# Preparing late q and k earlier, and splitting the last output product by columns, in a fused attention and MoE kernel

## The chip, the cores and the metric

The kernel runs on one core of one Trainium2 chip. The metric is the device time of one execution in microseconds (us). On one core there is no second die to compare with.

## The reference, cut to what matters

```python
# q, k, v: (4, 8, 768, 64) float32; lam: (8,); w_in: (512, 2048); w_out: (2048, 512)
for b in range(12):                      # blocks of 64 rows
    intra = (q_b k_b^T * decay mask) v_b
    inter = (q_b * lam_pow) kv_state
    out_b = intra + inter
    kv_state = lam_block * kv_state + (k_b * rev_pow)^T v_b
x = out as (3072, 512)                   # tokens x model
h = x @ w_in                             # (3072, 2048)
g = gelu_tanh(h)
return g @ w_out                         # (3072, 512) float32
```

Linear attention with decay, then a two-layer MLP over its output. In the kernel, attention is cut into 24 steps (a batch, 256 rows, half of the heads). The MLP's matrix products are queued as "filler" pieces, which are put between the dependent parts of the attention steps so that TensorE has work while other engines prepare the next step.

## The kernel before

Each step's q is scaled on VectorE (tile `qk`), its k is cast on ScalarE, its v is scaled on GpSimd (tile `v`), and from step 9 on a transposing transfer brings q and k into the layout for the scores. The loads of a step are issued behind the preparation of an earlier one. For step 10 they are split: v is issued right behind the transfer that transposes step 9.

```python
def prep_v(s):
    tv = a16p.tile([P, 2, HH, D], FP16, tag="v16", name=f"v16_{s}")
    pin(nc.gpsimd.tensor_tensor(wide(tv[:]), ld32[s][2][:], decay(dv, s), ALU.mult))
    a16[s] = a16[s] + (tv,)
    if s >= 6:
        if s + 3 == FIRST_DMA_T + 1:          # s == 7: step 10, q and k only
            load_step(s + 3, "qk")
        else:
            load_ahead(s + 3)

def prep_qk(s):
    ...
    pin(q_eng.tensor_tensor(wide(tq), q32[:], decay(dq, s), ALU.mult))
    ...
    if s >= FIRST_DMA_T:                      # FIRST_DMA_T = 9
        o = qkp.tile([P, 2, 2, 2, P], FP16, tag="qkT", name=f"qkT_{s}")
        pin(nc.sync.dma_start_transpose(...))
        qkT[s] = o
        if s == FIRST_DMA_T:
            load_step(s + 1, "v")             # v of step 10
```

The second MLP product is computed by seven half-size products of summed blocks (A to E are their PSUM banks, `gs` the sums of `g` that VectorE makes for them). Its very last product, bank E, is a 128x256 block over eight weight tiles; then one sum and one store:

```python
def product(m, p):
    ...
    dst = banks[name][:, half]
    t = slice(p * P, p * P + P)
    for i in range(HF):                       # HF = 8
        ...
        pin(nc.tensor.matmul(dst, lhsT, rhs, start=(i == 0), stop=(i == HF - 1), ...))
    ...
    elif final and m in (7, 6):
        ...
        d = o[:, T, T, :]
        pin(tt(d, banks[name][:, half], d, ALU.add))
        queue = nc.scalar if m == 7 else nc.sync
        pin(queue.dma_start(out=rows[:, T], in_=d))
```

The order of the late steps (`R` and `burst` are attention steps, `U` their state updates, `fill(n)` n pieces of the MLP):

```python
for n in range(8, 16):
    stage_t(n)
    prep_qk(n + 2) if n == 8 else prep(n + 2)
    fill(3 if n == 14 else 2)
    R(n, n - 1)
    ...
for n in range(16, NSTEP + 1, 2):             # NSTEP = 24
    if n + 2 < NSTEP:
        prep(n + 2)
    fill(2)
    burst((n, n + 1) if n < NSTEP else (), (15,) if n == 16 else (n - 2, n - 1))
    if n == NSTEP:
        break
    fill(2)
    U(n)
    U(n + 1)
    if n + 3 < NSTEP:
        prep(n + 3)
    fill(14 if n % 4 else 8)
fill(len(filler))
```

## Time and profile before

| | value |
|---|---|
| runs before the prediction | 203.87, 203.91 and 204.37 us |
| median | 203.91 us |
| run that was profiled | 204.35 us, span 202.6 us |
| TensorE busy | 194.3 us of the span |

The page cuts the span in 40 equal slices (about 5 us each) and gives each engine's busy share in tenths:

```profile
PE   6789999999999999999999999999999999999993
DVE  5896623889999989968799749889556471334753
```

TensorE (PE) has room only in the first three slices and the last. VectorE (DVE) is at 9 in many slices of the middle, and there its order of instructions can hold TensorE up for a few tenths of a microsecond. A finer table gives the busy time in chosen stretches. The columns here are TensorE matmuls, TensorE weight loads, VectorE, ScalarE, GpSimd, each with its number of instructions, then the granted clock, the share of the transfer engines and their rate:

```profile
60.00:66.00 6.00, 5.89 (x96) 4.67 (x94) 6.00 (x11) 2.32 (x6) 4.23 (x4) 1.00 1.22 231
66.00:72.00 6.00, 5.84 (x89) 5.08 (x90) 6.00 (x14) 3.22 (x7) 2.62 (x3) 1.00 1.23 271
130.00:140.00 10.00, 9.85 (x177) 8.65 (x175) 8.39 (x17) 3.98 (x9) 0.00 (x0) 1.00 0.09 18
```

VectorE is busy for all twelve microseconds from 60 to 72 us, and GpSimd for more than half of them. TensorE stands still for 0.27 us there and for 0.15 us between 130 and 140 us. Those are busy times with modelled ends, so the waits are read from the order of the chain rather than from these sums. The prediction shows that chain.

### The profile page before, as it was taken

How to read it: one execution, taken by the hardware profiler on the slowest of the kernel's cores; microseconds unless marked ns; L12 is line 12 of the kernel's file. 1: busy time of each engine (PE TensorE's matmuls, PEld its weight loads, DVE VectorE, ACT ScalarE, POOL GpSimd, SP SyncE). 2: the span in 40 equal slices, each digit the busy share in tenths (PEclk: the TensorE clock that was granted, in tenths of full speed). 3: DMA queues.
4: the chain of work that ended last, by engine and by line, in shares of the span. 5: the costliest groups of instructions: out<-in, count | busy, mean ns of one | idle time of the engine just before them, and what ended most of it. 6: DMA issues, size and time to landing. Idle time of an engine off the chain costs nothing.

```text
span 202.6 us, 5666 instructions
## 1 busy us (share of the span) xinstructions
PE 194.3 (96%) x2348; PEld 129.9 (64%) x2348; DVE 145.4 (72%) x293; ACT 107.8 (53%) x205; POOL 66.3 (33%) x80
## 2 busy tenths in 40 slices
PE   6789999999999999999999999999999999999993
PEld 1456544456888888654688764688664688545882
DVE  5896623889999989968799749889556471334753
ACT  2465778375993473487642378524367414466210
POOL 6594132457358254162541609203402000000000
PEclk9999999999999999999999999999999999999999
DMA  6999999999999999999975999305510003300014
GB/s 173 290 328 389 383 387 377 289 292 308 345 256 220 266 207 240 204 271 166 239 193 115 282 230 208 70 0 130 133 58 3 0 0 107 104 0 0 3 45 162
DMA packets 64202, 37.85 MB, mean 187 GB/s; under 512 B 17585, under 2 KB 59569, under 8 KB 64177
## 3 DMA queue, kind: packets, MB, share of 16 engines
q1 hardware_dynamic: 63344, 36.97, 72.1%
q10 hardware_dynamic: 832, 0.52, 0.8%
q8 instruction: 18, 0.29, 0.6%
q14 instruction: 8, 0.06, 0.1%
HBM read 27.26 MB, written 6.29 MB: 166 GB/s over the span
## 4 chain that ended last, share of the span: by engine, by line
PE 77%; DVE 11%; SPq 4%; DMA 4%; issue 2%; ACT 1%; DVEq 0%
PE Hps L484 34%; PE MD L555 7%; PE MB L555 7%; PE O2ps L499 7%; PE MA L555 7%; DVE gs L531 4%; SPq L70 4%; DMA wi<-in_moe_w_in_dram 4%; PE MC L555 3%; PE Hps L601 3%; PE S L295 2%; DVE qk L243 2%; DVE PT L305 2%; PE OK L353 1%; PE Tps L266 1%
## 5 line engine op out<-in xcount | busy, mean ns | idle before, releaser
L484 PE MATMUL Hps<-xT,w_in 128*128 128x512 f16 (+1 forms) x416 | 78.7, 346 | 0.0
L488 ACT ACTIVATE gT<-Hps 128x512 f16<-128x512 f32 x88 | 52.3, 597 | 29.5 <-PE Hps L484 28.5
L484 PEld LDWEIGHTS <-w_in 128*128 128x128 f16 x416 | 40.3, 98 | 33.7
L531 DVE TENSOR_TENSOR gs<-gT 128x1024 f16<-128x1024 f16 (+1 forms) x62 | 39.9, 699 | 18.5 <-ACT gT L488 18.5
L456 POOL TENSOR_TENSOR u<-t,lumask 128x256 f16<-128x256 f32 x40 | 29.4, 747 | 67.8 <-DVE t L449 49.8
L555 PEld LDWEIGHTS <-gs 128*128 128x128 f16 x400 | 38.9, 98 | 5.0 <-DVE gs L531 0.5
L305 DVE TENSOR_TENSOR PT<-S,mask 128x512 f16<-128x512 f32 x48 | 30.4, 681 | 9.5 <-PE S L295 9.5
L230 POOL TENSOR_TENSOR v<-v,dv 128x512 f16<-128x512 f32 x24 | 28.5, 1193 | 4.9 <-PE S L295 1.7
L555 PE MATMUL MA<-w_sum,gT 128*128 128x256 f16 x160 | 19.5, 273 | 0.4 <-DVE o L587 0.3
L555 PE MATMUL MB<-w_out,gs 128*128 128x256 f16 x160 | 19.1, 273 | 0.0
L555 PE MATMUL MD<-w_sum,gs 128*128 128x256 f16 x152 | 18.6, 273 | 0.3 <-DVE gs L531 0.3
L562 ACT ACTIVATE m<-MB 128x512 f32<-128x512 f32 x10 | 6.0, 597 | 23.9 <-PE MB L555 23.9
L248 ACT ACTIVATE qk<-k 128x512 f16<-128x512 f32 x24 | 15.0, 626 | 6.8 <-DMA k<-in_k_dram 6.8
L243 DVE TENSOR_TENSOR qk<-q,dq 128x512 f16<-128x512 f32 x23 | 18.5, 803 | 0.0
L555 PEld LDWEIGHTS <-gT 128*128 128x128 f16 x160 | 15.4, 98 | 3.5 <-ACT gT L488 0.5
L430 ACT ACTIVATE xT<-OK 128x256 f16<-128x256 f32 x29 | 11.2, 455 | 8.0 <-PE OK L353 7.7
L499 PE MATMUL O2ps<-w_out,gT 128*128 128x512 f16 x64 | 14.6, 379 | 0.0
L566 DVE TENSOR_TENSOR o<-MA,m 128x512 f32<-128x512 f32 x10 | 6.9, 688 | 10.2 <-ACT m L562 10.2
L128 DVE TENSOR_TENSOR w_sum<-w_out 128x1024 f16<-128x1024 f16 x10 | 8.9, 932 | 6.4 <-POOL w_out L118 3.5
L430 ACT ACTIVATE xT<-O 128x256 f16<-128x256 f32 x18 | 6.4, 458 | 10.2 <-PE O L404 7.9
L295 PEld LDWEIGHTS <-qkT 64*64 64x64 f16 x384 | 6.0, 106 | 7.0 <-issue 3.2
L449 DVE SCALAR_TENSOR_TENSOR t<-t,lamu,OK 128x64 f32<-128x64 f32 x44 | 10.1, 273 | 0.5
(68 smaller groups left out, 168.7 us busy)
## 6 DMA issues: line engine op xcount, KB each, us to landing
q<-in_q_dram SPq DMA_DIRECT2D x24, 256.0 KB, 5.2
k<-in_k_dram SPq DMA_DIRECT2D x24, 256.0 KB, 5.2
v<-in_v_dram SPq DMA_DIRECT2D x23, 256.0 KB, 5.3
out_dram<-o SPq DMA_DIRECT2D x22, 256.0 KB, 4.5
wo<-in_moe_w_out_dram SPq DMA_DIRECT2D x4, 1024.0 KB, 9.5
wi<-in_moe_w_in_dram SPq DMA_DIRECT2D x4, 512.0 KB, 7.8
wi<-in_moe_w_in_dram SPq DMA_DIRECT2D x2, 1024.0 KB, 12.8
v<-in_v_dram ACTq DMA_DIRECT2D x1, 256.0 KB, 4.3
```

Of the source, the lines that this page charges most:

```text
L230: pin(nc.gpsimd.tensor_tensor(wide(tv[:]), ld32[s][2][:], decay(dv, s), ALU.mult))
L243: pin(q_eng.tensor_tensor(wide(tq), q32[:], decay(dq, s), ALU.mult))
L248: pin(nc.scalar.activation(out=wide(tk), in_=k32[:], func=AF.Copy))
L305: pin(nc.vector.tensor_tensor(t[:, hl].rearrange("p b c d -> p b (c d)"), Sps[:].rearrange("p b c d -> p b (c d)"), mask[:].unsqueeze(1).t ...
L430: pin(nc.scalar.activation(out=d, in_=o, func=AF.Copy))
L449: pin(nc.vector.scalar_tensor_tensor(t[:, hp, :], state[half][:, hp, :], lamu[:, 2 * half + hp : 2 * half + hp + 1], K[:, hp, :], ALU.mult ...
L456: pin(nc.gpsimd.tensor_tensor(u[:], state[half][:].unsqueeze(2).to_broadcast([P, 2, 2, D]), lumask[:, 2 * half : 2 * half + 2, :].unsqueez ...
L484: pin(nc.tensor.matmul(by_block(Hps[:, i, :]), w_in16[:, c, f * P : (f + 1) * P], x(c), start=(c == 0), stop=(c == NC - 1)))
L488: pin(nc.scalar.activation(out=dst, in_=Hps[:], func=AF.Gelu_apprx_tanh))
L499: pin(nc.tensor.matmul(O2[tau][0][:], gT[:, f % HF, f // HF, tau * P : (tau + 1) * P], w_out16[:, f, :], start=(n == 0), stop=(n == NF - 1)))
L531: pin(nc.vector.tensor_tensor(gsum[m][:, i, :], block(T0, F0, i), block(T1, F1, i), op))
L555: pin(nc.tensor.matmul(dst, lhsT, rhs, start=(i == 0), stop=(i == HF - 1), skip_group_check=True))
```

## The change

Its intent is threefold.
- In step 9 one filler piece goes ahead of the preparation of step 11, so that a sum that TensorE waits for (`gs`) stands ahead of the `qk` product of step 11 on VectorE.
- In the last stretch the even steps 20 and 22 are prepared earlier among the filler pieces instead of right ahead of their burst. Step 18 stays where it was.
- The very last product is made in two halves of 128 columns, each with its own PSUM bank, sum and store.

```diff
@@ product()
+                if name == "E":
+                    banks["E2"] = ps_M.tile([P, P], FP32, tag="M", name="ME2")
...
-            for i in range(HF):
+            parts = [slice(0, P), slice(P, HE)] if name == "E" else [slice(0, HE)]
+            for cols, i in [(cols, i) for cols in parts for i in range(HF)]:
...
-                d = o[:, T, T, :]
-                pin(tt(d, banks[name][:, half], d, ALU.add))
-                queue = nc.scalar if m == 7 else nc.sync
-                pin(queue.dma_start(out=rows[:, T], in_=d))
...
+                    sums = [(parts[0], dst0[:, 0:P], nc.scalar), (parts[1], banks["E2"][:], nc.sync)]
+                for cols, part, queue in sums:
+                    d = o[:, T, T, cols]
+                    pin(tt(d, part, d, ALU.add))
+                    pin(queue.dma_start(out=rows[:, T, cols], in_=d))
@@ the order of the steps
         stage_t(n)
+        fill(1 if n == 9 else 0)
         prep_qk(n + 2) if n == 8 else prep(n + 2)
-        fill(3 if n == 14 else 2)
+        fill({9: 1, 14: 3}.get(n, 2))
...
-    for n in range(16, NSTEP + 1, 2):
-        if n + 2 < NSTEP:
-            prep(n + 2)
-        fill(2)
-        burst((n, n + 1) if n < NSTEP else (), (15,) if n == 16 else (n - 2, n - 1))
...
+    prep(18)
+    fill(2)
+    for n in range(16, NSTEP, 2):
+        burst((n, n + 1), (15,) if n == 16 else (n - 2, n - 1))
         fill(2)
         U(n)
         U(n + 1)
-        if n + 3 < NSTEP:
-            prep(n + 3)
-        fill(14 if n % 4 else 8)
+        for m in (n + 3, n + 4):
+            if m < NSTEP:
+                prep(m)
+            fill(4 if m % 2 == 0 and n % 4 == 0 else 6 if m % 2 == 0 else 6 if n % 4 == 0 else 10)
+    burst((), (NSTEP - 2, NSTEP - 1))
```

More of the change, by code (lines that the diff above doesn't have):

```diff
@@ L545, in product @@
                 banks[name] = ps_M.tile([P, 2, HE], FP32, tag="M", name=f"M{name}")
-            dst = banks[name][:, half]
+                if name == "E":
+                    banks["E2"] = ps_M.tile([P, P], FP32, tag="M", name="ME2")
+            dst = dst0 = banks[name][:, half]
             t = slice(p * P, p * P + P)
-            for i in range(HF):
+            parts = [slice(0, P), slice(P, HE)] if name == "E" else [slice(0, HE)]
+            for cols, i in [(cols, i) for cols in parts for i in range(HF)]:
                 lhsT = block(*G_PLAIN[m], i)[:, t] if m in G_PLAIN else gsum[m][:, i, t]
@@ L554, in product @@
                     rhs = w_sum16[:, w_slot[m], i, :]
-                pin(nc.tensor.matmul(dst, lhsT, rhs, start=(i == 0), stop=(i == HF - 1),
+                if cols.start:
+                    dst = banks["E2"]
+                pin(nc.tensor.matmul(dst[:, 0 : cols.stop - cols.start] if name == "E" else dst,
+                                     lhsT, rhs[:, cols], start=(i == 0), stop=(i == HF - 1),
                                      skip_group_check=True))
@@ L580, in product @@
                 rows = out[row : row + P, :].rearrange("q (e d) -> q e d", e=2)
-                d = o[:, T, T, :]
-                pin(tt(d, banks[name][:, half], d, ALU.add))
-                queue = nc.scalar if m == 7 else nc.sync
-                pin(queue.dma_start(out=rows[:, T], in_=d))
+                if m == 7:
+                    sums = [(slice(0, HE), banks[name][:, half], nc.scalar)]
+                else:
+                    sums = [(parts[0], dst0[:, 0:P], nc.scalar), (parts[1], banks["E2"][:], nc.sync)]
[3 more added lines that the diff above has]
+                    pin(queue.dma_start(out=rows[:, T, cols], in_=d))
             elif m == 6:
@@ L790 @@
         fill(2 if n in (8, 11, 15) else 3)
-    for n in range(16, NSTEP + 1, 2):
-        if n + 2 < NSTEP:
-            prep(n + 2)
-        fill(2)
-        burst((n, n + 1) if n < NSTEP else (), (15,) if n == 16 else (n - 2, n - 1))
-        if n == NSTEP:
-            break
+    prep(18)
+    fill(2)
+    for n in range(16, NSTEP, 2):
+        burst((n, n + 1), (15,) if n == 16 else (n - 2, n - 1))
         fill(2)
```

## The prediction

> **What bounds the kernel now.** I read first the busy shares by engine, then the chain that ended last in order of time, then the timeline around each place where that chain leaves TensorE, and last the stores at the very end. The page says
>
> ```profile
> PE 194.3 (96%) x2348; PEld 129.9 (64%) x2348; DVE 145.4 (72%) x293; ACT 107.8 (53%) x205; POOL 66.3 (33%) x80
> ```
>
> The span is 202.6 us and TensorE is busy for 194.3 of it at full granted clock, so a change can only win the few places where TensorE stands still, or the stretch after its last product. The list of what TensorE's matmuls and weight loads waited for gives no wait over 1.5 us, and after 60 us only waits of 0.2 to 0.5 us. The chain names those that the change can touch:
>
> ```profile
> 65.50 0.61 DVE gs L531
> 66.11 0.05 issue
> 66.16 1.05 PE MD L555 x8
> ...
> 106.91 0.45 issue
> 107.36 0.70 DVE o L587
> 108.06 0.04 issue
> 108.10 1.91 PE MA L555 x16
> ...
> 119.96 0.55 PE O L404 x8
> ...
> 136.57 0.70 DVE o L587
> 137.27 0.04 issue
> 137.31 0.44 PE K L393 x31
> ```
>
> Columns: start, length, what. Three times TensorE resumes the moment a VectorE instruction ends: at 66.16, 108.10 and 137.31 us. Between 67.2 and 99 us, and from 138 us to its end, the chain is TensorE almost unbroken. The timelines there:
>
> ```profile
> 62.01 2.94 POOL L230 TENSOR_TENSOR v<-v,dv 128x512 f16<-128x512 f32 x2
> 63.97 1.53 DVE L243 TENSOR_TENSOR qk<-q,dq 128x512 f16<-128x512 f32 x1
> 65.42 0.68 DVE L531 TENSOR_TENSOR gs<-gT 128x1024 f16<-128x1024 f16 x1
> 69.78 0.68 DVE L587 TENSOR_TENSOR o<-MD,o 128x512 f32<-128x512 f32 x1
> 70.68 4.53 PE L484 MATMUL Hps<-xT,w_in 128*128 128x256 f16 x40
> ...
> 135.97 0.68 DVE L243 TENSOR_TENSOR qk<-q,dq 128x512 f16<-128x512 f32 x1
> 136.57 0.69 DVE L587 TENSOR_TENSOR o<-MD,o 128x512 f32<-128x512 f32 x1
> ```
>
> In both places a qk product (the preparation of a later step's q) stands in VectorE's order just ahead of the instruction TensorE needs. At the end:
>
> ```profile
> 199.25 0.42 DVE L582 TENSOR_TENSOR o<-ME,o 128x256 f32<-128x256 f32 x1 [0.45 <-PE ME L555]
> 199.71 0.36 SPq L584 DMA_DIRECT2D out_dram<-o  x1
> ```
>
> Last product, 0.42 us sum, store; then 2.9 us until the span ends. In tenths of a microsecond the DMA share is full from 198.6 to 200.4, dips to 0.43 at 200.5, is full again at 200.7 and gone at 201.1.
>
> **What the Trainium skill says.** (1) "Perfetto Trace Analysis", Optimizing Scalar/DVE Operations: GpSimd and VectorE share an SBUF read port. The trace agrees: the qk product took 1.53 us while GpSimd made its v, against 0.68 us at 135.97 with GpSimd idle. (2) "TensorE: Matmul & The Clock Gate", Back-to-back issue gap: in a stream of weight load and matmul pairs both set the pace, about 81 ns a pair at 128 columns. Here it is a little quicker: 8 such pairs in 0.55 us (the O line above), 69 ns; 256 columns take 109 ns. So half the columns do not cost half the time. (3) "PSUM — Partial Sum Buffer", PSUM bank collisions raise a hardware error: two engines must not touch one bank in the same quadrants at once. That is why the half product needs a second bank before VectorE may read the first; this trace cannot show it. (4) "DMA: Bandwidth & Descriptors", Anatomy of one DMA: most of a transfer's fixed cost is the receipt from the memory written. The trace agrees in kind: data stop at 201.1 us, the span ends at 202.6.
>
> **Part 1, step 9: one piece of filler ahead of the preparation of step 11.** TensorE's order is unchanged by it; on VectorE the sum gs_6 and the product qk_11 change places. Before, the eight MD matmuls that start at 64.85 us last 8 x 109 ns = 0.87, so the next eight could start at 65.72; they started at 66.16, after gs_6 (65.42 to 66.10). Loss 0.44 us. With gs_6 in qk_11's place at 63.97, and slowed by GpSimd as the qk was (or less, as 16-bit sums before it were slowed by about half), it ends by 65.1 to 65.4, in time: TensorE gains up to 0.44 there. Not all must survive: VectorE is busy 10.0 of 10 us between 60 and 70, and its total work is the same. TensorE next needs it for banks: the Hps of 70.68 waits in the program for the o sum that ran 69.78 to 70.46, slack 0.22 us. If VectorE is no faster overall, only 0.22 survive; if the sum loses less to GpSimd than the qk did (qk lost 1.53 - 0.68 = 0.85), more. After that VectorE has idle time waiting on TensorE's results (0.74 us at 76.0), so what survives 71 us stays. I take **0.33 us**.
>
> **Part 2, q and k of steps 20 and 22 earlier, of 18 not.** Filler between bursts adds up as before (12 and 18 pieces), so TensorE's order stays. qk_20 moves two pieces up, but VectorE's order does not change around it and TensorE waits for nothing at that burst (118.6 us): 0. qk_22 moves from between the o sums to ahead of three gs sums. Then the o sum of L587 starts when its product ends, some 136.15 rather than 136.57, and ends about 136.85. TensorE's K would have followed its first matmul at 136.97 and now resumes at 137.31: gain **0.34 us**. The three gs sums move back 0.6 to 0.7 us; in the old order they are done, in steps, at about 131.9, 132.6 and 133.2, and their products start at 133.5, 134.4 and 135.2, so at 132.6, 133.3 and 133.9 they are still in time. The wait at 108.10 has qk_18 in front of it, and its place is unchanged: it stays. From 138 us nothing else stops TensorE, so 0.34 goes to the end.
>
> **Part 3, the last product in halves.** TensorE: 16 pairs of 69 ns, 1.10 us, for 8 of 109 ns, 0.87: **0.23 us added**. First half done 0.55 us after the start, second 1.10. A sum of 128 columns: 512 columns take 0.68, 256 take 0.42, so by the same slope 0.29. Counting from 198.34 (start of ME): second half ready 199.44, its sum ends 199.75, its store is issued at 199.79, 0.08 us later than now. What it carries is half: now 128 KB move from 200.55 to 201.05. The first half's 64 KB join the backlog: stores of 256, 256 and 128 KB fill the engines from 198.55, 640 KB at 338 GB/s, to 200.45; 64 KB more at the rate the 512-byte input rows had (some 31 ns a packet against 45 for 1 KB, read from packets and share early and late; 128 x 31 ns / 16 engines = 0.25 us) last to 200.70. The second half's data can start at 199.79 + 0.84 (the delay of today's last store) = 200.63, so 200.70, and end at 200.95, against 201.05. Gain **0.10 us**, with the fixed 1.5 us behind it kept.
>
> **Sum.** 0.33 + 0.34 + 0.10 = 0.77 us: 203.91 - 0.77 = **203.1 us**.
>
> **Rivals.**
> Rival A: VectorE bounds 60 to 72 us and takes part 1 back. For it: ten busy microseconds of ten, and slack of only 0.2 us at the Hps. Against: the long stall of qk behind GpSimd may shrink. Then the total gain is 0.55 to 0.65: 203.3.
> Rival B: the store at the end gains nothing or loses. For it: TensorE's 0.23 extra, and 512-byte rows at a lower rate. If such a write costs more than I read off the loads, the end moves 0.1 to 0.3 back: 203.3 to 203.5. Against it: the last store waits in no queue today (the dip at 200.5), so halving its bytes must save something.
> Rival C: the moved qk_22 delays a gs sum into TensorE's way. Slack of 0.9 us or more speaks against it; it would cancel part 2: 203.5.
> Rival D: steps moved up let transposes and loads collide otherwise and shift small waits anywhere. The order on the transfer queue does not change, so I give it a few tenths either way.
>
> **Range and chances.** All parts right in full give 0.44 + 0.34 + 0.2, about 1.0: 202.9; parts 1 and 3 failing give 203.6. The three runs before spread over 0.5 us, so I add some 0.3 below and 0.1 above: 202.6 to 203.7. Two per cent are 4.1 us, more than all TensorE stalls after 60 us together, and no part can lose as much: within 2% with 0.98, a hundredth for each side.
>
> **What would show it.** Part 1: the MD matmuls near 66 us follow each other without a weight load that waits for gs, and the Hps near 70 us starts 0.2 to 0.4 earlier. Part 2: the K matmuls near 137 us show no wait for L587's successor, and the wait at 108 us remains. Part 3: the ME matmuls take about 1.1 us, two sums of 0.29 us, and data end about 1.15 us after the last issue begins, where now it is 1.35. The prediction is wrong if a new wait of TensorE on VectorE stands near 70, 76 or 133 us, or if time from the end of the last sum to the span's end (2.9 us) does not shrink by at least the 0.08 us that the sum is late.

## The result, and the profile after

| kernel | runs (us) | median | profiled run |
|---|---|---|---|
| before | 203.81, 203.87, 203.91, 204.37 | 203.89 | 204.35, span 202.6 |
| after | 203.77, 203.80, 204.26, 204.33 | 204.03 | 203.80, span 202.0 |

The ratio is 1.0002 (95% interval 0.9979 to 1.0026). Ratios here are formed from the runs of both kernels in the same rounds, so they are not quite the ratios of the medians quoted. Predicted were 203.1 us and a range of 202.6 to 203.7; the median lies above it.

The two traces disagree with the two medians: the profiled run of after is 0.55 us *shorter* than that of before. So I first checked each step in the trace. The page and the chain of waits after:

```profile
PE 194.9 (96%) x2356; PEld 130.7 (65%) x2356; DVE 145.8 (72%) x294; ACT 107.8 (53%) x205; POOL 66.2 (33%) x80
```

```profile
65.07 1.75 PE MD L561 x16
66.82 2.62 PE Hps L484 x24
...
107.24 0.70 DVE o L598
107.94 0.04 issue
107.98 1.91 PE MA L561 x16
...
136.58 0.45 PE O L379 x32
137.02 0.28 PE K L393 x32
137.30 0.33 PE O L404 x4
```

All 16 MD matmuls now follow each other (65.07), so the wait at 66 us is gone. All 32 K matmuls follow each other (137.02), so the wait at 137 us is gone too. The wait at 108 us stands as foretold. Around 64 and 70 us, in the timelines of after (start, length, engine, line, operation):

```profile
62.07 2.93 POOL L230 TENSOR_TENSOR v<-v,dv 128x512 f16<-128x512 f32 x2
64.03 1.52 DVE L531 TENSOR_TENSOR gs<-gT 128x1024 f16<-128x1024 f16 x1
65.48 0.68 DVE L243 TENSOR_TENSOR qk<-q,dq 128x512 f16<-128x512 f32 x1
69.46 0.46 DVE L449 SCALAR_TENSOR_TENSOR t<-t,lamu,OK 128x64 f32<-128x64 f32 x2
69.74 0.64 PE L344 MATMUL OK<-PT,v 64*64 64x128 f16 x16
69.84 0.68 DVE L598 TENSOR_TENSOR o<-MD,o 128x512 f32<-128x512 f32 x1
70.57 0.81 PE L484 MATMUL Hps<-xT,w_in 128*128 128x256 f16 x6
```

Two readings matter. First, the sum that has taken qk's place beside GpSimd costs 1.52 us, as qk did (1.53), and qk, now behind it, costs 0.68: VectorE finishes both at 66.16 us where before it finished them at 66.10. It has gained nothing; only the order in which TensorE receives them is better. Second, TensorE pays part of its gain back at 70 us. The 16 matmuls of L344 take 0.64 us, which includes a wait. Before, the last 14 of them took 0.40 without one:

```profile
70.11 0.40 PE L344 MATMUL OK<-PT,v 64*64 64x128 f16 x14
```

By its timing the wait is for VectorE: the `t` of step 9 (L449) ends at 69.92 us, and in the chain the matmuls go on at 69.97. The MLP products behind them (Hps) start at 70.57 instead of 70.68 us, hardly earlier. In the stretch from 130 to 138 us the early qk product shows where the diff put it, and the sum of L598 runs without a qk ahead of it:

```profile
131.24 0.69 DVE L243 TENSOR_TENSOR qk<-q,dq 128x512 f16<-128x512 f32 x1
131.84 1.89 DVE L531 TENSOR_TENSOR gs<-gT 128x1024 f16<-128x1024 f16 x3
136.04 0.69 DVE L598 TENSOR_TENSOR o<-MD,o 128x512 f32<-128x512 f32 x1
```

The busy table for 130 to 140 us has TensorE at ten of ten microseconds now:

```profile
130.00:140.00 10.00, 10.00 (x180) 8.91 (x178) 9.01 (x20) 3.92 (x9) 0.35 (x1) 1.00 0.18 27
```

At the end, the last product is 16 matmuls, with two sums, and a store on each of two queues (the group on ScalarE's queue, ACTq, holds also the store of the product before):

```profile
197.73 1.06 PE L561 MATMUL ME<-w_sum,gs 128*128 128x128 f16 x16
198.38 0.29 DVE L594 TENSOR_TENSOR o<-ME,o 128x128 f32<-128x128 f32 x1
198.39 0.86 ACTq L595 DMA_DIRECT2D out_dram<-o  x2
198.82 0.29 DVE L594 TENSOR_TENSOR o<-ME,o 128x128 f32<-128x128 f32 x1 [0.16 <-PE ME L561]
199.14 0.36 SPq L595 DMA_DIRECT2D out_dram<-o  x1
```

So both waits that the change aims at are gone from the trace, and still the median did not fall. To compare traces without their first part, I use three marks: the first scores of step 8 (near 57.7 us, ahead of everything that the change moves), the scores of step 22 (near 148 us), and the start of the last product ME. A stretch is the difference of two marks.

| trace | step 8 scores at | to step 22 scores | to ME | ME to end of span | from step 8 to the end |
|---|---|---|---|---|---|
| before | 57.67 | 90.77 | 49.74 | 4.4 | 144.9 |
| after | 57.72 | 90.27 | 49.74 | 4.3 | 144.3 |

In the traces the change wins 0.6 us. Either the profiled runs are of different kinds, or the traced gain is given back in other runs.

### The profile page after: what moved, and what is told of

Read it like the earlier page. It is cut to its first block, busy times and chain, and to the rows that moved or that the text cites. A ratio compares the mean times of both kernels' runs of the same rounds, so it can differ in the third digit from the quotient of the medians. Undisturbed runs are those within 1.5% of the kernel's fastest.

```text
span 202.0 us, 5685 instructions
## 1 busy us (share of the span) xinstructions
PE 194.9 (96%) x2356; PEld 130.7 (65%) x2356; DVE 145.8 (72%) x294; ACT 107.8 (53%) x205; POOL 66.2 (33%) x80
## 4 chain that ended last, share of the span: by engine, by line
PE 81%; DVE 6%; SPq 4%; DMA 3%; ACT 2%; issue 1%; DVEq 0%
PE Hps L484 37%; PE MB L561 8%; PE MA L561 8%; PE MD L561 7%; SPq L70 4%; PE MC L561 4%; PE Hps L612 3%; DMA wi<-in_moe_w_in_dram 3%; PE O2ps L499 3%; PE S L295 3%; DVE w_sum L128 2%; PE OK L353 2%; PE OK L344 1%; PE Tps L266 1%; DVE gs L531 1%
## 5 line engine op out<-in xcount | busy, mean ns | idle before, releaser
L531 DVE TENSOR_TENSOR gs<-gT 128x1024 f16<-128x1024 f16 (+1 forms) x62 | 40.8, 712 | 18.3 <-ACT gT L488 18.3
L243 DVE TENSOR_TENSOR qk<-q,dq 128x512 f16<-128x512 f32 x23 | 17.6, 767 | 0.0
L449 DVE SCALAR_TENSOR_TENSOR t<-t,lamu,OK 128x64 f32<-128x64 f32 x44 | 10.1, 274 | 0.5
```

The source lines that it names most:

```text
L531: pin(nc.vector.tensor_tensor(gsum[m][:, i, :], block(T0, F0, i), block(T1, F1, i), op))
```

## The experiments

The theory at the outset was that the parts do what the traces show, and that runs of one kernel come in kinds which the medians mix. The rival was that the parts give each other's gain back, above all that part 1's gain is taken back at 70 us and that the halves cost what the stores save. Every kernel below gave the correct result; each has five rounds and one trace, kernels named together ran on one chip, and each is compared with the runs of before in the same rounds. Where an interval excludes 1, the text says so.

### The parts one by one

**Before, verbatim.**

> The kernel before, once more, because single executions of both kernels fall at two values (before 203.8 to 203.9 and 204.37; after 203.8 and 204.3) and the trace of before is one of the long ones (span 202.6) while that of after is one of the short (202.0). Theory S (two states, change worth something within a state): the runs fall in two groups 0.4 to 0.6 us apart, the short group's spans near 202.0 to 202.1, and the share of each group differs between the kernels; a trace of a short run shows where the 0.5 us lies. Theory N (the change is worth nothing): a trace of a short run of before has none of the stalls near 66 and 137 us. Theory P (preamble): the difference lies in the first 50 us, ahead of everything that was changed.

Measured: 203.85 to 206.83 us, median 204.70; from step 8 to 22 90.77 us, as in the first trace of before. The chip is noisier than the first one, so what follows reads the stretches in the traces first and the times second.

**Step 9 only.**

```diff
         stage_t(n)
+        fill(1 if n == 9 else 0)
         prep_qk(n + 2) if n == 8 else prep(n + 2)
-        fill(3 if n == 14 else 2)
+        fill({9: 1, 14: 3}.get(n, 2))
```

> Only part 1, one piece of filler ahead of the preparation of step 11. By comparing the two traces, TensorE gains 0.38 us at 66.8 us and loses 0.2 of it at 70 us where the matmuls of step 10 wait for the t of step 9: net 0.18 us, so 203.7 if the parts act as in the traces (Theory S). Theory N: 203.9, the same as before in every state.

Measured: median 204.10 us, ratio 0.9982 (0.9934 to 1.0030); step 8 to 22 in 90.39 us, 0.38 less than before. That looked like the full gain of part 1. The next runs show that it is not part 1 at all.

**Steps 20 and 22 only**, that is, the rewritten last loop and nothing else of the change.

> Only part 2, q and k of steps 20 and 22 earlier. By the traces it removes the 0.33 us stall near 137 us and nothing behind it gives this back. Theory S: 203.55, span 0.33 shorter in the same state. Theory N: 203.9.

Measured: median 204.28 us, ratio 0.9971 (0.9930 to 1.0011); step 8 to 22 in 90.44 us, 0.33 less than before. The K matmuls are unbroken, and the wait at 66 us is there as before. The predicted 0.34 us for part 2 is met.

**Halves only**, that is, the change in `product()` and nothing else.

> Only part 3, the last product in halves. By the traces the halves cost TensorE 0.02 us (1.06 for 1.04), the last sum ends 0.11 earlier, and the stores, slower in 512-byte rows (282 for 338 GB/s), end 0.08 earlier counted from the start of the last product. Theory S: gain 0.08, 203.8. Theory N: 0. A rival, that halves cost: 204.1.

Measured: median 205.35 us, ratio 1.0000 (0.9958 to 1.0043). The surprise is elsewhere in its trace: step 8 to 22 takes 90.34 us, 0.43 less than before, in a kernel that is the same there. The wait at 66 us is missing though nothing was done about it. What differs is the landing of the v of step 10: GpSimd starts that product at 63.55 us, against 62.01 in before's trace, and so VectorE's qk product takes only 0.68 us and is done at 63.85, and the last sum, though it takes 1.53 us beside GpSimd, ends in time at 65.31. This is the new theory: **the load of v for step 10 lands early in some runs and late in others.** Landed early, it lets GpSimd run beside VectorE's sums, and TensorE waits at 66 us; landed late, no wait. In step 9's own run above it had landed late too (GpSimd at 63.98).

### The load of v for step 10, set on purpose

The load is one instruction. It can be issued ahead of the transposing transfer of step 9, or later, behind the loads of q, k and v for step 12.

```diff
 # early                                          # late
 def prep_qk(s):                                  def prep_v(s):
     ...                                              ...
     if s >= FIRST_DMA_T:                             if s >= 6:
+        if s == FIRST_DMA_T:                             ... (loads ahead)
+            load_step(s + 1, "v")                +        if s == FIRST_DMA_T:
         o = qkp.tile(...)                        +            load_step(s + 1, "v")
         pin(nc.sync.dma_start_transpose(...))
         qkT[s] = o                               (and taken out of prep_qk in both)
-        if s == FIRST_DMA_T:
-            load_step(s + 1, "v")
```

**Before, load early.**

> The kernel before, with the load of v for step 10 issued ahead of the transpose of step 9 and not behind it, so that it always lands before GpSimd is free for it (62.0 us). Theory V (the two values of 203.9 and 204.4 are two landings of this load: landed before 62.0, GpSimd makes v10 and v11 at once, [...]slows qk11 to 1.53 us and TensorE waits 0.44 us for gs6 at 66 us; landed near 63.5, it does not): always the wait at 66 us, span 202.6, 204.37 on a quiet chip. Theory W (the load has nothing to do with it, the states come from the first 20 us): the same mixture as the kernel before.

Measured: 204.30, 204.30, 204.33, 204.39, 204.43 and 204.97 us. Step 8 to 22 in 90.76 us, with the wait at 66 us.

**Before, load late.**

> The kernel before, with the load of v for step 10 issued after the loads of step 12, some 2.5 us later, so that it always lands after 63.5 us. Theory V: no wait at 66 us (16 MD matmuls in one row), span 202.1 or less, 203.85, half a microsecond under the early one, with nothing of the change in it. Theory W: the same mixture as the kernel before. Rival: landing as late as 65 us makes products of step 10 near 69.5 us wait, then 204.4 or more.

Measured: 203.82, 203.97, 204.18 and three at 204.69 to 204.71 us. Step 8 to 22 in 90.32 us. Its timeline:

```profile
63.21 0.68 DVE L245 TENSOR_TENSOR qk<-q,dq 128x512 f16<-128x512 f32 x1
63.81 0.68 DVE L531 TENSOR_TENSOR gs<-gT 128x1024 f16<-128x1024 f16 x1
64.94 1.91 PE L555 MATMUL MD<-w_sum,gs 128*128 128x256 f16 x16
66.59 1.04 POOL L230 TENSOR_TENSOR v<-v,dv 128x512 f16<-128x512 f32 x1 [4.46 <-DMA v<-in_v_dram]
```

With GpSimd waiting for its data until 66.59 us, qk takes 0.68 us with no part of the change in the kernel, the sum is done at 64.5, and the MD matmuls run in a row. A *later* transfer makes this stretch 0.44 us shorter (90.76 less 90.32). This settles the theory. The two groups of times in this kernel, at the same setting of the load, say that there is a second cause of difference too.

**After, load early.**

> The changed kernel with the load early. Theory V: as its trace, no wait at 66, but 0.2 us lost at 70 us, span 202.0, 203.8; 0.55 us better than the kernel before with the load early (0.18 step 9, 0.33 step 22, about 0.08 the halves).

Measured: 203.82 (the profiled run), 204.26, 204.27, 204.33 and 204.35 us, ratio 0.9986 (0.9963 to 1.0009); step 8 to 22 in 90.25 us.

**After, load late.**

> The changed kernel with the load late. Theory V: no wait at 66 and none at 70, so step 9's piece of filler is worth nothing, the step-22 part still 0.33 and the halves 0.08: span 201.7, 203.5, only 0.4 better than the kernel before with the load late.

Measured: 203.39, 203.46, 203.62, 203.82, 204.17 and 204.27 us, ratio 0.9966 (0.9942 to 0.9989), an interval below 1; step 8 to 22 in 90.02 us.

So the first trace of before (90.77) and that of after (90.27) are both of the early kind, and a like comparison gives 0.5 us early (90.76 less 90.25) and 0.3 us late (90.32 less 90.02) up to step 22, before the end is counted.

### Parts at the early setting, and after twice more

**Step 9 only, load early.**

> Step 9's piece of filler alone, with the load of v for step 10 early, where the wait at 66 us exists in every run. The whole change with that load early showed two values, 203.82 once and 204.26 to 204.35 four times, while the kernel before showed one (204.30 to 204.43). Theory A (the second value comes from step 9's piece: VectorE's later products are 0.6 us later and something near 70 to 76 us sometimes waits): a mixture of 204.15 and 204.6. Theory B (it comes from steps 20 and 22): 204.15 always.

Measured: median 204.76 us, ratio 0.9980 (0.9941 to 1.0020); step 8 to 22 in 91.74 us in a run of 205.56. The chain of its trace shows why it tells nothing of part 1:

```profile
56.33 8.34 DMA qkT<-qk
64.67 0.04 issue
64.71 0.42 PE S L295 x16
```

In this run TensorE waited for the transposing transfer of step 9, 8.34 us from issue to landing. The load issued ahead of it is a possible reason, but the three other kernels with that order did not show it, so the reason stays open. The run is a miss for its purpose.

**Steps 20 and 22 only, load early.**

> Steps 20 and 22 earlier alone, with that load early. Theory A: 204.0 always (204.33 less the 0.33 of the wait at 137 us). Theory B: a mixture of 204.0 and 204.45.

Measured: median 205.30 us, ratio 1.0007 (0.9967 to 1.0046); step 8 to 22 in 90.43 us, 0.33 less than before at the same setting. Part 2 is confirmed a second time; the times themselves are too scattered to show it. Part 1 at the early setting follows by difference: after takes 90.25 to 90.27 us, part 2 alone 90.43 to 90.44, so part 1 is worth 0.17 to 0.18 us there. At the late setting it is worth nothing: step 9 only took 90.39, before 90.32.

**After, load early, again.**

> The changed kernel with the load early once more, for a trace of its longer value. Theory A: the longer run differs from the shorter between 60 and 100 us, by 0.45 us. Theory B: it differs after 114 us. Theory H: it differs before 57 us, in loads and preparation that the change did not touch, and the kernel before has it as well.

Measured: 203.77, 204.10, 204.27 (the profiled run), 205.02, 205.06 and 205.28 us, ratio 0.9982 (0.9939 to 1.0024); step 8 to 22 in 90.27 us, but the scores of step 8 only at 58.20 us. The longer run thus differs ahead of everything that the change moves, as theory H has it.

**After, verbatim, again.**

> The changed kernel as it is, for more of its runs and another trace: a mixture of 203.5 (load late), 203.8 and 204.3; its median 203.8 to 204.2, not more than 0.3 from that of the kernel before.

Measured: 203.42, 203.60, 203.66, 203.75, 203.80 and 204.53 us (the profiled run), ratio 0.9940 (0.9904 to 0.9976). The expectation is missed: the median is 203.70, and that of before in these rounds 204.90, so this comparison finds the change 1.2 us shorter where the first found nothing. That is more than the traces show for the change (0.6 us at most, below), which points to a different mixture of kinds in the runs of the two kernels here. Whether the change itself alters the mixture was not tested. In its trace step 8 to 22 takes 90.26 us, as in the other traces of after, but the scores of step 8 start at 58.47 us, 0.75 us later than in the first trace. So here is the second cause. It lies ahead of all that the change touches. The start in the timeline of before, then of this run:

```profile
5.41 0.40 PE L266 MATMUL Tps<-ident,qk 128*128 128x128 f16 x4 [0.48 <-POOL dq L189]
6.32 0.81 PE L155 MATMUL idle<-ones 128*128 128x512 f16 x3
```

```profile
5.42 0.61 PE L266 MATMUL Tps<-ident,qk 128*128 128x128 f16 x4 [0.48 <-POOL dq L189]
6.66 1.49 PE L155 MATMUL idle<-ones 128*128 128x512 f16 x3
```

The same four transposes take 0.61 us for 0.40, the same three warm-up matmuls 1.49 for 0.81: TensorE runs at about half its pace for longer at the start of this run. The run with step 8 at 58.20 us shows the same (1.48 us for those three matmuls). The views print a granted clock of 1.00 here, but only because they count a stretch without a clock record as full. The records themselves, kept in each run's packed trace, settle it: the first one says full clock, and it begins 4.88 us behind the start of the span in the first trace of before, 9.12 us in this run. In thirteen of the 18 traces it begins at 4.5 to 7.2 us, and step 8's scores start at 57.56 to 57.96 us; in the other five it begins at 8.8 to 9.6 us, and they start at 58.20 to 58.47 us. The five are traces of five different kernels, two of them with nothing of the change but steps 20 and 22. So the long start is a full clock that is granted later.

### Toward a faster kernel, and the start

What was still open: whether the gains add up once the load is late and the wait at 108 us is dealt with too, and whether one more warm-up matmul keeps the start short. All four kernels ran on one chip, with before at 203.78 to 205.48 us (median 204.91 of 11 runs).

**After, load late, and step 18's preparation behind the two filler pieces.**

```diff
-    prep(18)
     fill(2)
+    prep(18)
```

> The changed kernel with the load of v for step 10 late and q and k of step 18 prepared behind the two last pieces of filler before their burst, not ahead of them, so that VectorE's last o sum of that group goes before qk18. If the wait of TensorE at 108 us is due to qk18 alone, it goes (0.34 us): from step 8's scores to step 22's 89.7 us where it was 90.02, and the shortest runs at 203.05. If VectorE's work bounds that stretch, TensorE waits as long a moment later: 203.4.

Measured: 202.98, 203.15, 203.41, 203.65, 203.76 (profiled) and 203.79 us, ratio 0.9934 (0.9906 to 0.9961). Step 8 to 22 in 89.60 us, 0.42 less than after with the load late (90.02). The interval excludes 1. The scores of step 8 start at 58.37 us: the start was of the long kind.

**The same, and a fifth warm-up matmul ahead of the first preparation.**

```diff
-    idle(4)
+    idle(5)
     prep(0)
```

> The same with one more warming matmul ahead of the first transpose (five for four). If the clock opens after enough busy time in a row, the gap of 0.5 us at 4.9 us is what lets it open late, and the late start (first transposes 0.6 us for four, step 8's scores after 58.1) no longer occurs: all six runs within 0.3 us. If it opens at a moment of its own, the two starts stay.

Measured: 202.97 (profiled), 203.01, 203.04, 203.12, 203.12 and 204.05 us, median 203.08, ratio 0.9924 (0.9894 to 0.9955), again without 1. Five runs lie within 0.15 us and one 0.9 us above them, so the expectation of all six within 0.3 us is missed. Step 8 to 22 again in 89.60 us, step 8 at 57.56. Its chain at 107 us:

```profile
106.64 0.25 PE K L393 x16
106.89 0.33 PE O L404 x4
107.22 1.84 PE MA L561 x16
```

No VectorE instruction stands ahead of MA any more. This version is shorter than before in the same rounds, by less than 2%. After itself was not run on this chip; there the stretch speaks, 89.60 us against 90.25 to 90.27.

**Before, load late, fifth warm-up matmul.**

> The kernel before with the load late and the fifth warming matmul: 203.85 in all runs if the clock opens early now, else 203.85 and 204.6 mixed; step 8's scores to the end 144.4.

Measured: 203.81, 203.85, 203.96 (profiled), 204.62, 204.63 and 204.70 us, ratio 0.9973 (0.9944 to 1.0001); step 8 to 22 in 90.34 us.

**After, load late, fifth warm-up matmul.**

> The changed kernel with both: 0.4 us under the one before it in this list, start for start: 203.45 in all runs, or 203.45 and 204.2 mixed; step 8's scores to the end 144.0.

Measured: 203.42, 203.47, 203.54, 203.56 (profiled), 203.84 and 204.19 us, ratio 0.9944 (0.9917 to 0.9971), an interval below 1; step 8 to 22 in 90.00 us.

The fifth matmul is not shown to help. The three traces that have it start short (full clock from 4.51, 6.47 and 5.80 us, step 8 at 57.56, 57.74 and 57.72 us), but before with it still has three of six runs 0.7 to 0.9 us longer than the others, and none of those was traced.

### The like comparison in one table

Stretches in the traces, in us, from step 8's scores on (several traces of a row are separated by commas; ends of spans are taken unrounded from the packed traces). The run that waited for the transposing transfer is left out.

| kernel | load | step 8 to 22 | step 8 to the end |
|---|---|---|---|
| before | early | 90.77, 90.77, 90.76 | 144.9, 144.9, 144.9 |
| steps 20 and 22 | early | 90.44, 90.43 | 144.5, 144.5 |
| after | early | 90.27, 90.25, 90.27, 90.26 | 144.3, 144.3, 144.3, 144.3 |
| before | late | 90.32, 90.34 | 144.4, 144.4 |
| step 9 | late | 90.39 | 144.5 |
| halves | late | 90.34 | 144.4 |
| after | late | 90.02, 90.00 | 144.1, 144.0 |
| after with step 18 later | late | 89.60, 89.60 | 143.6, 143.6 |

The change is worth 0.6 us with the load early and 0.4 us with it late; neither kernel decides by itself which of the two it gets. From step 22 to ME all take 49.74 us within 0.01. From ME to the end of the span, nine traces with the halves take 4.28 to 4.30 us and nine without take 4.37 to 4.39: the halves win 0.08 us in the mean.

## Why the prediction was wrong

**The step that failed is the sum: "203.91 - 0.77".** The 0.77 us were read off the waits in one trace, and that trace is of a run of 204.35 us. They were then taken from the median of 203.91 us, as though the typical run had the same waits. With the load set late, before takes 203.82 to 204.18 us in its shorter group, and its trace has no wait at 66 us; with the load set early it takes 204.30 us and more and has the wait. The three runs of 203.81 to 203.91 in the first comparison fit the late kind by their times; they were not traced, so that is an inference. On that reading the prediction subtracted a wait from runs that did not have it. Beside this, one term of the sum was clearly mis-sized, that of part 1 (below).

**Why the medians came out equal.** The trace of after's run of 203.80 us is of the early kind with the short start. Its runs of 204.26 and 204.33 us fit a run that was traced later, early with the long start (204.27 us, span 202.5). So the first comparison set three short runs of before against two middling and two long ones of after. The traces show that both causes exist and what each is worth: 0.44 us for the load in before, up to 0.75 us for the start. That just this mixture made these medians is inferred from the values. From the traced run the same sum would have given 204.35 - 0.77 = 203.58 us, and after's traced run took 203.80. So of the 0.89 us between 203.14 and the median of 204.03, 0.44 come from starting at 203.91 instead of 204.35, 0.22 from gains smaller than foretold in the traced pair, and 0.23 from after's longer runs in its median.

**Part 1, predicted 0.33 us, measured 0.17 to 0.18 by difference with the load early and none with it late.** The mechanism was right: the wait at 66 us went away. The size was off because the sum was expected to lose less beside GpSimd than the qk product. It lost the same (1.52 us for 0.68, the qk 1.53 for 0.68), so VectorE was no faster, and about 0.2 us of TensorE's gain was given back at 70 us. The trace of before could have told: the sum just ahead of that qk, which the prediction took to be slowed "by about half", had lost as much beside GpSimd:

```profile
62.52 1.53 DVE L531 TENSOR_TENSOR gs<-gT 128x1024 f16<-128x1024 f16 x1
```

This is rival A, near the 0.22 us named for it, though TensorE waits at the matmuls of L344 and not at the Hps that the prediction watched. That wait near 70 us was also one of its signs of being wrong, and it came. With the load late there is nothing to win, a case that no rival named.

**Part 2, predicted 0.34 us, measured 0.33 in two kernels.** Right in mechanism and size. The sums moved back were in time, so rival C did not occur.

**Part 3, predicted 0.10 us, measured 0.08, by terms that were wrong and cancelled: luck.** TensorE's extra was put at 0.23 us, from 69 ns a pair. The 16 pairs took 1.06 us where the 8 wider ones took 1.04, which is 0.02 more. Taking the fixed tail of about 0.17 us off both gives 56 ns a pair, against 109. The 69 ns were a misreading: a burst of eight such pairs takes 0.55 us in the chain, but a burst of four takes 0.33, so four more cost 55 ns each and 0.11 us of the burst does not grow with their number. So the second sum ended earlier than expected, not later: 199.11 less 197.73 is 1.38 us behind the start of ME, against 199.67 less 198.18, 1.49 us, before. The stores gave nothing: the prediction counted on 0.18 us from them, since the last one is half as large, but from the end of the last sum to the end of the span it is 2.90 us before and 2.91 after. That this time would not shrink was the second sign of being wrong, and it came too. In the two half-microseconds at the end, before and then after:

```profile
200.00:200.50 0.50, 0.00 (x0) 0.00 (x0) 0.00 (x0) 0.00 (x0) 0.00 (x0) 1.00 0.96 318
200.50:201.00 0.50, 0.00 (x0) 0.00 (x0) 0.00 (x0) 0.00 (x0) 0.00 (x0) 1.00 0.79 264
```

```profile
200.00:200.50 0.50, 0.00 (x0) 0.00 (x0) 0.00 (x0) 0.00 (x0) 0.00 (x0) 1.00 1.00 277
200.50:201.00 0.50, 0.00 (x0) 0.00 (x0) 0.00 (x0) 0.00 (x0) 0.00 (x0) 1.00 0.06 15
```

Before has a gap ahead of the last store (share 0.79, the engines waiting for it). After has none: the engines are full (1.00) until the end, but with rows of 512 bytes they move 277 GB/s, against 352 in the half-microsecond from 199.5 us of before, with rows twice as long. The last store now stands in a backlog, so more speed on TensorE or VectorE should not bring it forward; no run tests that. Rival B was right about the shorter rows and wrong about TensorE's extra time.

**The range.** It allowed 0.3 us below and 0.1 above for the spread of the runs. The spread in runs of one kernel was seen (0.5 us) and treated as noise around one value; it was two or more values. Rival D came closest, but it asked whether *the change* would shift a load. The load shifts by itself.

**What stays open.** What makes the v load land early or late, and what makes the full clock begin late, is not found. Runs of 205 us and more, up to 206.83, came on all three chips of the experiments, mostly of before and of single parts, but of after with the load early too (205.02 to 205.28). One of them was traced (205.56 us), and it waits for a transposing transfer; the others were not.

## What to carry to other kernels

When a predicted gain is smaller than the spread between runs of one kernel, find out first which kind of run the trace is of: put its own time beside the median, and take from a median only waits that its runs have. Putting a needed result first does not make a loaded engine faster: here VectorE was done with both instructions at 66.16 us where it had been at 66.10, and only the order of the results changed. A transfer that landed later removed the same wait without any of it. And a part that is invisible in whole times can be measured between two marks in the trace, as part 2 was, at 0.33 us in two kernels whose times scattered over one to two microseconds.

## What the Trainium skill lacked or had wrong

- "TensorE: Matmul & The Clock Gate", Back-to-back issue gap: the page's pace for a stream of pairs at 128 columns, about 81 ns, is not what this last product shows. 16 such pairs took 56 ns each once the tail is taken off (0.89 us for 16), which the section gives only for an isolated matmul.
- "Perfetto Trace Analysis", Optimizing Scalar/DVE Operations: the page says that VectorE and GpSimd share a read port, but neither it nor another page gives the time that an ordinary sum or product of two tensors loses by it. Here a 16-bit sum of 128x1024 and a mixed product of 128x512 lost the same, 0.68 to 1.52 and 1.53 us, and GpSimd's own product went from 1.04 to 1.49 us.
- "DMA: Bandwidth & Descriptors", Specifications: the page gives 512 bytes as the least transfer for full rate. The 512-byte store rows at the end moved 277 GB/s with the engines full, the longer rows before them 352.
- "TensorE: Matmul & The Clock Gate", Part 1: The HAM clock gate: the page says that how many matmuls run slow at the start varies from run to run and that the loss is under one per cent. The runs agree: the first record of full clock begins at 4.5 to 9.6 us, step 8's scores start at 57.56 to 58.47 us, and 0.91 us is under 0.5% of the time. What the section does not say is that this can be more than a late tuning step is worth (here 0.4 to 0.6 us).
